# Normalized blocks in the feature maps' buffer, and tail additions moved on VectorE

## The chip, the cores and the metric

The kernel runs on one core of a Trainium2 chip. The metric is the device time of one execution in microseconds (us), the median of the timed runs. The profile is of one further execution on the same kind of chip, taken by the hardware profiler; its times are in us from the first instruction. The engines are PE (TensorE), DVE (VectorE), ACT (ScalarE), POOL (GpSimd) and SP (SyncE), which here only issues DMAs.

## The reference

The input x has 2048 rows of 640 columns, in bfloat16. It is normalized by row, xn = (x - mean) / sqrt(var + 1e-5), and goes into two branches whose product is added back:

```python
def reference(...):
    xn = _layernorm(x, axis=-1)
    s = _A_ref(xn, A_wq, A_wk, A_wv, A_wo, A_beta)                          # attention with a memory
    g = _silu(_B_ref(xn, B_w_gate, B_w_up, B_w_down))                       # gated feed-forward, 640 -> 1536 -> 640
    return x + s * g
```

Branch A has 32 heads of 20 columns and cuts the sequence into 4 segments of 512 rows. In each segment it makes causal softmax attention (a_dot) and a linear read of a memory, num / den with num = phi(q) M and den = phi(q) z, where phi(t) is t + 1 for t > 0 and exp(t) otherwise. The two are mixed by a gate per head; then M and z get this segment's phi(k) and v added. The mixed output is multiplied by wo. Branch B is sigmoid(xn w_gate) * (xn w_up), multiplied by w_down.

## The kernel before

The kernel goes through the 4 segments (n = 0 to 3, 512 rows each). While the attention of segment n runs, slot by slot, the dense work of both branches and the preparation of segment n + 1 are woven in between. The whole order of each engine's instructions is written out by hand: the schedule is manual, an event is put at a slot number with a fraction (the table TIMES), there are 20 slots to a segment, and the PE work that hangs on no due time (gate, up and down products) fills the time between by a planner's costs. So each engine executes its instructions in the order in which the Python code issues them, and a wait of one instruction holds everything behind it on that engine.

Preparing segment m = n + 1 (during segment n): `stats` makes mean and variance, `norm` at slots 5.26, 5.72, 6.03 and 6.29 makes one normalized block of 128 rows each (`ln_norm`, L243, on VectorE), and after each `ln_spill` (L265) stores it from SP's queue into the DRAM scratch Xd, 160 KB. At slot 7.22 `ln_dmaT` (L269) loads all of Xd transposed into xnT. The projections of K (from slot 9.69), Q and V on PE read xnT (L282 and L284 are their evictions).

The normalized blocks lie in a ring of two buffers named xn, so the third and the fourth block of a segment are written into the buffers of the first and the second, after their spills have ended.

The feature maps phi are made in place on ktok and qt by `phi_min` (L360 and L361, VectorE: the minimum with zero into a tile "mn", then the maximum with zero in place), `phi_exp` (L365, ScalarE) and `phi_end` (L369, VectorE). "mn" has one buffer of 1536 columns. In a segment the maps of K come at slots 7.15 to 8.3 and 12.77 to 13.77, those of Q from 16.0 to 19.18. Ahead of segment 0 the same tile serves as the operand of PE's warm-up products.

Gate and up products: `do_gate` ends in a tanh on ScalarE (L421), `do_up` in the product hT on VectorE (L432). `do_down` gives yp on PE, a tanh on ScalarE (L448) and the product aa on VectorE (L449); it is a generator, so that its 12 products can be interleaved with other work. All these accumulate in a ring of four PSUM buffers (tag "d"), which an eviction on ScalarE or VectorE sets free. Attention: `scores` (L541, PE), the exponentials (L549, ScalarE), the masks (L551, GpSimd), the products with V (L565, PE), and then on VectorE the transposes L573 and L585 with the reciprocal L576 between them.

The tail is that of segment 3. The attention output oT (5 chunks of 128 rows) is loaded by L474, L477 and L507 from DRAM, and the memory's part oTm is added by `out_add` (L481): the chunks 0 to 2 at slot 19.86 (one instruction of 1536 columns), chunk 3 at slot 20.9. Chunk 4 is made by `tail_T4` twice, for two blocks of 128 rows each: two transposes on PE (L513), a copy of the lower half by ScalarE (L517), and an addition on VectorE (L518) of o6, which L508 loads. Two down products of the last block of rows ("held") are kept back to give PE work meanwhile. Then come the eight output products of `tail_piece` (L525), each of five matmuls that take the chunks of oT in order, each followed by a product on VectorE (L527), with additions and stores (`tail_add`, L533 and L536).

Of the kernel before, what the change touches and what calls it, by code (L numbers as in the profile page):

```python
# [9 lines left out]
P = 128  # L10
D = 640
# [3 lines left out]
NSEG = 4  # L15
L = 512
F = 1536
DC = D // P
# [6 lines left out]
BF = mybir.dt.bfloat16  # L25
F32 = mybir.dt.float32
ACT = mybir.ActivationFunctionType
ALU = mybir.AluOpType
# [22 lines left out]
def segment_units(n):  # L51
# [6 lines left out]
    turn=(0.03, 0.27, 1.29), turn_last=(0.0, 0.135, 0.43), attend=0.36, last=(0.36, 0.75), rest=350, dot6=0.43, load6=0.48,  # L58
    dot7=1.92, load7=1.95, add=(4.27, 4.52), out=(5.25, 5.95, 7.25, 8.35, 8.74, 9.06, 9.45, 11.05), update=-1.2,
    mem=(2.23, 4.32, 3.0, 6.98, 6.98, 2.45, 9.09, 10.79), mem_spill=11.56, mem_T=14.4, mem_T_last=12.63,  # L60
    k_tok=2.04, dot3=13.22, dot5=17.84, load5=18.1, add5=19.86, dot6_last=19.55, load6_last=19.6, add6_last=20.9, stats0=(0.53, 0.9, 1.65, 3.6),
    stats=(-0.55, 0.13, 1.32, 3.57), norm=(5.26, 5.72, 6.03, 6.29), norm_T=7.22, ready=12.0,
    K=(9.69, 10.07, 10.49, 13.82, 14.29), Q=(11.32, 11.72, 12.29, 12.45, 13.52), K_eng='vaava', Q_eng='avvav',
    V=(10.33, 13.33, 14.43, 14.63, 17.05, 17.66, 19.78, 20.06), V_eng='avaavvav', k_spill0=14.77, k_lay0=15.15,
# [11 lines left out]
def kernel(  # L76
# [14 lines left out]
    nc = tc.nc  # L91
# [5 lines left out]
    ps_d = ctx.enter_context(tc.tile_pool(name="ps_d", bufs=4, space=PSUM))  # L97
    lnp = ctx.enter_context(tc.tile_pool(name="ln", bufs=2))
    stg = ctx.enter_context(tc.tile_pool(name="stg", bufs=1))
# [8 lines left out]
    Xd = [dpool.tile([L, D], BF, name=f"Xd{i}") for i in range(2)]  # L108
# [9 lines left out]
    xt_of, xnT_of = {}, {}  # L118
# [120 lines left out]
        nc.gpsimd.tensor_tensor(rs[:, sl], rs[:, sl], mhalf[:, sl], op=ALU.pow)  # L239

    def ln_norm(n, j, mv, rs):
        xn = lnp.tile([P, D], BF, name="xn", bufs=2)
        nc.vector.tensor_scalar(xn[:], xt_of[n][:, j, :], mv[:, j, 0:1], rs[:, j:j + 1],  # L243
                                op0=ALU.subtract, op1=ALU.mult)
        return xn

    def ln_tiles(n):
        mv = lnp.tile([P, 4, 2], F32, name="mv")
        rs = lnp.tile([P, 4], F32, name="rs")
        return mv, rs  # L250
# [11 lines left out]
            nc.vector.tensor_copy(dst, pT[:])  # L262

    def ln_spill(n, j, xn):
        nc.sync.dma_start(Xd[n % 2][j * P:(j + 1) * P, :], xn[:])  # L265

    def ln_dmaT(n):
        xnT_of[n] = xpool.tile([P, DC, L], BF, name="xnT")
# [2 lines left out]
    seg = {}  # L271
# [181 lines left out]
    def finish(steps):  # L453
        for _ in steps:
            pass
# [23 lines left out]
    def out_add(n, c0, c1):  # L479
        oT = seg[n]["oT"][:, c0:c1, :]  # L480
        nc.vector.tensor_tensor(oT, oT, seg[n]["oTm"][:, c0:c1, :], op=ALU.add)  # L481
# [19 lines left out]
    HALF = P // 2  # L501
    o6 = cpool.tile([HALF, L], BF, name="o6")
    nc.gpsimd.memset(o6[:].bitcast(mybir.dt.uint32), 0)

    def tail_load():
        src = OTd[(NSEG - 1) % 2]
        nc.sync.dma_start(seg[NSEG - 1]["oT"][R5 - C3:P, 3, :], src[R5:C4, :])  # L507
        nc.sync.dma_start(o6[0:R6 - C4, :], src[C4:R6, :])  # L508

    def tail_T4(j0, j1):  # L510
        po = ps_d.tile([P, 2, P], BF, name="po", tag="d")
        for j in range(j0, j1):
            nc.tensor.transpose(po[:, j - j0, :], seg[NSEG - 1]["odot"][:, j, C4:D], ident[:])  # L513
        t = slice(j0 * P, j1 * P)
        oT = seg[NSEG - 1]["oT"][:, DC - 1, t]
        pf = po[:].rearrange("p j t -> p (j t)")
        nc.scalar.copy(oT[HALF:P, :], pf[HALF:P, :])  # L517
        nc.vector.tensor_tensor(oT[0:HALF, :], pf[0:HALF, :], o6[:, t], op=ALU.add)  # L518

    def tail_piece(j, half):  # L520

        s, hs = seg[NSEG - 1], slice(half * HD, (half + 1) * HD)
        sp = ps_d.tile([P, HD], F32, name="sp", tag="d")
        for c in range(DC):
            nc.tensor.matmul(sp[:], lhsT=s["oT"][:, c, j * P:(j + 1) * P], rhs=Wo[:, c, hs],  # L525
                             start=(c == 0), stop=(c == DC - 1), skip_group_check=True)
        nc.vector.tensor_tensor(s["aa"][j][:, hs], s["aa"][j][:, hs], sp[:], op=ALU.mult)  # L527
# [108 lines left out]
    mv, rs = ln_tiles(0)  # L636
# [26 lines left out]
    def norm0(j):  # L663
        if j < 2:
            nc.vector.reciprocal(rs[:, j:j + 1], rs[:, j:j + 1])
        xns[j] = ln_norm(0, j, mv, rs)
# [82 lines left out]
    held = [dense.pop() for _ in range(2)]  # L749
# [9 lines left out]
    def at(t, ns, fn, *a):  # L759
        events.append((t, len(events), ns, lambda: fn(*a)))  # L760

    visits = {}
    for p in range(0, OLD, 5):
        n, g = units[p][0], units[p][1][0][0]
# [36 lines left out]
    def norm(m, j):  # L801
        ln_spill(m, j, ln_norm(m, j, st["mv"], st["rs"]))

    EVAC = dict(v=nc.vector, a=nc.scalar)
    for n in range(NSEG):
        t0 = n * SEG

        def on(name, ns, fn, *items):
            times = TIMES[name]
            for i, it in enumerate(items):  # L810
                at(t0 + (times[i] if isinstance(times, (list, tuple)) else times), ns, fn, *it)

        if n >= 1:
            on("dot6", 0, dot_spill, (n - 1, 4, 7))
            on("load6", 0, out_load, (n - 1, 0, C4))
            on("dot7", 0, dot_spill, (n - 1, 7, 8))
            on("load7", 0, out_load, (n - 1, C4, D))
            if n >= 2:
                on("add", 0, out_add, (n - 1, 0, DC - 1), (n - 1, DC - 1, DC))
            on("out", V_NS, out_item, *[(n - 1, i) for i in range(8)])  # L820
            on("update", 700, m_update, (n - 1,))
            on("mem", MEM_NS, mem_part, *[(n, i % 4, i // 4) for i in range(8)])
            on("mem_spill", 0, mem_spill, (n,))
            on("mem_T_last" if n == NSEG - 1 else "mem_T", 0, mem_T, (n,))
            if n < NSEG - 1:
                on("k_tok", 0, k_tok, (n,))
        on("dot3", 0, dot_spill, (n, 0, 4))
        if n == NSEG - 1:
            on("dot5", 0, dot_spill, (n, 4, 6))
            on("load5", 0, out_load, (n, 0, 6 * 4 * DH))  # L830
            on("add5", 0, out_add, (n, 0, 3))
            on("dot6_last", 0, dot_spill, (n, 6, 7))
            on("load6_last", 0, tail_load, ())
            on("add6_last", 0, out_add, (n, 3, 4))
            continue
        m = n + 1
        on("stats0" if n == 0 else "stats", 0, stats, *[(m, j) for j in range(4)])
        on("norm", 0, norm, *[(m, j) for j in range(4)])
        on("norm_T", 0, ln_dmaT, (m,))
        on("ready", 0, ready.add, (m,))  # L840
        at(t0 + TIMES["K"][0] - 0.001, 0, new_seg, m)
        on("K", GLU_NS, do_K, *[(m, c, EVAC[TIMES["K_eng"][c]]) for c in range(DC)])
        on("Q", GLU_NS, do_Q, *[(m, c, EVAC[TIMES["Q_eng"][c]]) for c in range(DC)])
        on("V", V_NS, do_V, *[(m, i // 2, i % 2, EVAC[TIMES["V_eng"][i]]) for i in range(8)])
        on("k_spill0", 0, spill, (m, 0, nc.sync, None))
        on("k_lay0", 0, relayout, (m, 0, Kd, KT, nc.sync))
        on("q_spill0", 0, spill, (m, 0, None, nc.sync))
        on("q_lay0", 0, relayout, (m, 0, Qd, QT, nc.sync))
        on("q_spill1", 0, spill, (m, 1, None, nc.sync))
        on("k_spill1", 0, spill, (m, 1, nc.sync, None))  # L850
        on("q_abs", 0, q_abs, (m, 0, 3), (m, 3, DC))
        on("bound", 0, bound, (m,))
        on("bound_mm", C_NS, bound_mm, (m,))
        on("bound_lay0", 0, bound_dma, (m, 0))
        at(t0 + SEG - 0.003, 0, relayout, m, 1, Kd, KT, nc.sync)
        at(t0 + SEG - 0.002, 0, relayout, m, 1, Qd, QT, nc.sync)
        at(t0 + SEG - 0.001, 0, bound_dma, m, 1)
        for name, sg, key in (("phi_k", n, "ktok"), ("phi_q", m, "qt")):
            for i, (c0, c1) in enumerate(((0, 2), (2, 4 if key == "ktok" else 5))):
                for fn, t, a in zip((phi_min, phi_exp, phi_end), TIMES[name][i], ((sg, key, c0, c1), (), ())):  # L860
                    at(t0 + t, 0, fn, *a)
        if n + 2 < NSEG:
            on("load_x", 0, load_x, (n + 2,))
# [31 lines left out]
    def fill(want):  # L895
        while done < want and (cur[0] is not None or dense and may(dense[0][0])):
            step()
# [26 lines left out]
        if cur[0] is not None and cur[0][0] * cur[0][1] < TIMES["rest"]:  # L924
            complete()
    fill(1e12)
    for k in (1, 0):
        for _ in range(9):
            next(held[k][3])
        tail_T4(2 - 2 * k, 4 - 2 * k)  # L930
        finish(held[k][3])
    tail_piece(0, 0)
    tail_piece(0, 1)
    tail_add(0, 0, 2, nc.gpsimd, nc.sync)
# [41 lines left out]
```

## Time and profile before

| | |
|---|---|
| median of 3 timed runs | 319.3 us (319.18, 319.30, 320.31) |
| the profiled execution's own time | 320.84 us |
| its span, first to last instruction | 319.0 us |
| mean granted TensorE clock | 0.998 |
| PE busy | 308.1 us, 97% |
| weight loads (beside PE) | 167.8 us, 53% |
| VectorE busy | 226.1 us, 71% |
| ScalarE busy | 226.7 us, 71% |
| GpSimd busy | 134.7 us, 42% |
| DMA | 41.27 MB, mean 129 GB/s |

A line of the list of waits names the waiting engine, the tile and line that it waited to write or run, what released it, and then us in total, how many times, and the longest. A line of the chain in order of time gives its start, its length and what it was; the chain is followed back from the last instruction, at each step to what released it. A line of the timeline gives start, length, engine, line, operation, output and inputs, and in brackets the idle time before it. The ends of matmuls are modelled, so a run of matmuls seems to last somewhat longer than PE needs until the next can start. Engines read a tile's name without its buffer number; "o" in a row of L518 is o6.

### The profile page before, as it was taken

How to read it: one execution, taken by the hardware profiler on the slowest of the kernel's cores; microseconds unless marked ns; L12 is line 12 of the kernel's file. 1: busy time of each engine (PE TensorE's matmuls, PEld its weight loads, DVE VectorE, ACT ScalarE, POOL GpSimd, SP SyncE). 2: the span in 40 equal slices, each digit the busy share in tenths (PEclk: the TensorE clock that was granted, in tenths of full speed). 3: DMA queues.
4: the chain of work that ended last, by engine and by line, in shares of the span. 5: the costliest groups of instructions: out<-in, count | busy, mean ns of one | idle time of the engine just before them, and what ended most of it. 6: DMA issues, size and time to landing. Idle time of an engine off the chain costs nothing.

```text
span 319.0 us, 10222 instructions
## 1 busy us (share of the span) xinstructions
PE 308.1 (97%) x4297; PEld 167.8 (53%) x4327; DVE 226.1 (71%) x507; ACT 226.7 (71%) x228; POOL 134.7 (42%) x231
## 2 busy tenths in 40 slices
PE   7999999989999999899999999999999999999995
PEld 4544445655445445554566454545466655444673
DVE  5474455655868986978869999979686776744475
ACT  3724478769798777767898777678987676777730
POOL 1880035534263444434445364344444353525313
PEclk9999999999999999999999999999999999999999
DMA  7985886230642364513964443419534100180202
GB/s 235 388 312 147 293 216 167 85 84 2 178 151 81 106 123 117 125 43 123 206 177 143 132 104 115 113 69 214 179 94 128 32 23 24 62 165 26 83 23 84
DMA packets 55246, 41.27 MB, mean 129 GB/s; under 512 B 25952, under 2 KB 53824, under 8 KB 55200
## 3 DMA queue, kind: packets, MB, share of 16 engines
q1 hardware_dynamic: 52656, 35.87, 40.8%
q10 hardware_dynamic: 2544, 4.75, 4.0%
q8 instruction: 34, 0.56, 0.7%
q14 instruction: 12, 0.10, 0.1%
HBM read 19.98 MB, written 14.73 MB: 109 GB/s over the span
## 4 chain that ended last, share of the span: by engine, by line
PE 86%; DMA 7%; DVE 3%; issue 1%; ACT 1%; POOL 1%; SPq 0%; DVEq 0%; ACTq 0%
PE up L124 10%; PE psq L124 10%; PE gp L124 9%; PE yp L124 9%; PE Sps L541 8%; PE gp L128 6%; PE up L128 5%; PE ApsT L565 5%; PE psv L124 5%; PE yp L128 4%; PE psq L128 4%; DMA Xd<-xn 4%; PE sp L124 3%; PE psv L128 2%; DMA xnT<-Xd 2%; PE sp L128 2%
## 5 line engine op out<-in xcount | busy, mean ns | idle before, releaser
L549 ACT ACTIVATE pt<-Sps 128x2048 bf16<-128x2048 f32 x80 | 150.2, 1878 | 40.6 <-PE Sps L541 39.8
L551 POOL TENSOR_SCALAR_AFFINE_SELECT pt<-pt 128x512 bf16<-128x512 bf16 x128 | 83.6, 669 | 158.5 <-ACT pt L549 155.8
L432 DVE SCALAR_TENSOR_TENSOR hT<-tg,up 128x512 bf16<-128x512 bf16 x48 | 32.5, 677 | 23.8 <-PE up L124 10.0
L124 PE MATMUL up<-xnT,Wu 128*128 128x512 bf16 x146 | 40.3, 380 | 2.7 <-DVE hT L432 1.3
L124 PE MATMUL gp<-xnT,Wg 128*128 128x512 bf16 x146 | 38.9, 379 | 0.6 <-issue 0.5
L421 ACT ACTIVATE tg<-gp 128x512 bf16<-128x512 f32 x48 | 28.6, 595 | 14.3 <-PE gp L124 10.0
L124 PE MATMUL yp<-Wd,hT 128*128 128x320 bf16 x246 | 38.2, 300 | 0.0
L541 PE MATMUL Sps<-QT,KT 23*128 23x384 bf16 (+3 forms) x512 | 32.1, 301 | 0.1
L124 PEld LDWEIGHTS <-hT 128*128 128x128 bf16 x246 | 22.7, 98 | 11.3 <-issue 3.0
L573 DVE STREAM_TRANSPOSE tb<-ApsT 128x512 f32<-128x512 f32 x31 | 22.0, 710 | 3.4 <-PE ApsT L565 3.3
L128 PE MATMUL gp<-xnT,Wg 128*32 128x512 bf16 x352 | 24.4, 380 | 0.0
L124 PEld LDWEIGHTS <-Wu 128*128 128x128 bf16 x159 | 14.3, 98 | 18.7 <-issue 5.3
L565 PE MATMUL ApsT<-pt,V 128*32 128x512 bf16 (+2 forms) x496 | 23.5, 299 | 0.0
L124 PEld LDWEIGHTS <-Wg 128*128 128x128 bf16 x152 | 14.1, 98 | 15.8 <-issue 1.9
L449 DVE SCALAR_TENSOR_TENSOR aa<-t,yp 128x320 bf16<-128x320 bf16 x32 | 15.2, 475 | 9.8 <-ACT t L448 9.6
L128 PE MATMUL yp<-Wd,hT 128*32 128x320 bf16 x552 | 21.9, 300 | 0.0
L128 PE MATMUL up<-xnT,Wu 128*32 128x512 bf16 x324 | 21.8, 380 | 0.0
L541 PEld LDWEIGHTS <-KT 23*128 23x128 bf16 x512 | 9.3, 92 | 23.6 <-issue 23.4
L585 DVE STREAM_TRANSPOSE obT<-ob 128x256 f32<-128x256 f32 x31 | 13.4, 433 | 11.0 <-POOL ob L582 10.9
L582 POOL TENSOR_TENSOR ob<-tb,rb 128x320 bf16<-128x320 f32 x27 | 19.7, 731 | 2.2
L124 PE MATMUL psq<-xnT,Wq 128*128 128x512 bf16 x82 | 19.4, 379 | 0.2
L124 PE MATMUL psv<-Wv,xnT 128*128 128x320 bf16 x115 | 18.8, 302 | 0.5 <-ACT xnT L661 0.4
(123 smaller groups left out, 444.3 us busy)
## 6 DMA issues: line engine op xcount, KB each, us to landing
KT<-Kd SPq DMA_DIRECT2D x32, 80.0 KB
QT<-Qd SPq DMA_DIRECT2D x32, 80.0 KB
out_dram<-xt SPq DMA_DIRECT2D x14, 160.0 KB
Wg<-in_B_w_gate_dram ACTq DMA_DIRECT2D x1, 1920.0 KB
Wu<-in_B_w_up_dram ACTq DMA_DIRECT2D x1, 1920.0 KB
xt<-in_A_x_dram SPq DMA_DIRECT2D x3, 640.0 KB
Wd<-in_B_w_down_dram SPq DMA_DIRECT2D x1, 1920.0 KB
Xd<-xn SPq DMA_DIRECT2D x12, 160.0 KB
```

What stands on the lines that cost most here:

```text
L124: nc.tensor.matmul(out_, lhsT=lhsT, rhs=rhs, start=start, stop=stop, skip_group_check=True)
L128: nc.tensor.matmul(out_[cols], lhsT=lhsT[:, cols], rhs=rhs, start=start, stop=stop, tile_position=(0, 32 * r), skip_group_check=True)
L421: nc.scalar.activation(tg[:], gp[:], ACT.Tanh, scale=0.5)
L432: nc.vector.scalar_tensor_tensor(out=h[:], in0=seg[n]["tg"][:], scalar=1.0, in1=up[:], op0=ALU.add, op1=ALU.mult)
L449: nc.vector.scalar_tensor_tensor(out=s["aa"][j][:, hs], in0=t2[:], scalar=1.0, in1=yp[:], op0=ALU.add, op1=ALU.mult)
L541: nc.tensor.matmul(Sps[:, r, c0:c0 + ncol], lhsT=KT[32 * r:32 * r + DH + 3, g, kb * P:(kb + 1) * P], rhs=QT[32 * r:32 * r + DH + 3, g, q0: ...
L549: nc.scalar.activation(pt[:, :, 0:ntot], Sps[:, :, 0:ntot], ACT.Exp, scale=SCALE)
L551: nc.gpsimd.affine_select(out=pt[:, :, c0:c0 + P], in_=pt[:, :, c0:c0 + P], compare_op=ALU.is_ge, fill=0.0, base=0, pattern=[[0, 4], [1, P ...
L565: nc.tensor.matmul(ps[32 * r:32 * r + 32, q0:L], lhsT=Vflat[n % 2][:, off:off + 32], rhs=t[:, r, c0:c0 + ncol], start=(i == 0), stop=(i == ...
L573: nc.vector.transpose(tb[:].rearrange("p h e -> p (h e)"), ps[:].rearrange("p (a t b) -> p a b t", t=32, b=2))
L582: eng.tensor_tensor(to, of, by, op=ALU.mult)
L585: nc.vector.transpose(s["obT", g // 4][:, g % 4, :].bitcast(F32), ob[:].rearrange("p a e b -> p (a e b)").bitcast(F32))
```

## The change

Two edits that do not touch each other.

First, for the segments 1 to 3, the first two normalized blocks (j = 0 and 1) are written side by side into one tile "mn" of the feature maps' buffer (2 x 640 of its 1536 columns), taken anew for each segment. The ring of two xn buffers holds the blocks 2 and 3 alone (and all four of segment 0). The spills and the transposing load stay as they are.

Second, in the tail the addition of chunk 3 is taken out of the table of events, and the additions L518 out of `tail_T4`. All three are issued on VectorE after both pairs of transposes and after the end of the first held down product, directly ahead of the end of the second held down product and of the output products.

```diff
     def ln_norm(n, j, mv, rs):
-        xn = lnp.tile([P, D], BF, name="xn", bufs=2)
-        nc.vector.tensor_scalar(xn[:], xt_of[n][:, j, :], mv[:, j, 0:1], rs[:, j:j + 1],
+        if n > 0 and j < 2:
+            if j == 0:
+                seg["xn"] = stg.tile([P, 3 * L], BF, name="mn")
+            xn = seg["xn"][:, j * D:(j + 1) * D]
+        else:
+            xn = lnp.tile([P, D], BF, name="xn", bufs=2)[:]
+        nc.vector.tensor_scalar(xn, xt_of[n][:, j, :], mv[:, j, 0:1], rs[:, j:j + 1],
                                 op0=ALU.subtract, op1=ALU.mult)
         return xn
...
+    tail_po = {}
+
     def tail_T4(j0, j1):
-        po = ps_d.tile([P, 2, P], BF, name="po", tag="d")
+        po = tail_po[j0] = ps_d.tile([P, 2, P], BF, name="po", tag="d")
         for j in range(j0, j1):
             nc.tensor.transpose(po[:, j - j0, :], seg[NSEG - 1]["odot"][:, j, C4:D], ident[:])
+        nc.scalar.copy(seg[NSEG - 1]["oT"][HALF:P, DC - 1, j0 * P:j1 * P],
+                       po[:].rearrange("p j t -> p (j t)")[HALF:P, :])
+
+    def tail_add4(j0, j1):
         t = slice(j0 * P, j1 * P)
-        oT = seg[NSEG - 1]["oT"][:, DC - 1, t]
-        pf = po[:].rearrange("p j t -> p (j t)")
-        nc.scalar.copy(oT[HALF:P, :], pf[HALF:P, :])
-        nc.vector.tensor_tensor(oT[0:HALF, :], pf[0:HALF, :], o6[:, t], op=ALU.add)
+        nc.vector.tensor_tensor(seg[NSEG - 1]["oT"][0:HALF, DC - 1, t],
+                                tail_po[j0][:].rearrange("p j t -> p (j t)")[0:HALF, :], o6[:, t], op=ALU.add)
...
-            on("add6_last", 0, out_add, (n, 3, 4))
...
-    for k in (1, 0):
-        for _ in range(9):
-            next(held[k][3])
-        tail_T4(2 - 2 * k, 4 - 2 * k)
-        finish(held[k][3])
+    for _ in range(9):
+        next(held[1][3])
+    tail_T4(0, 2)
+    finish(held[1][3])
+    for _ in range(9):
+        next(held[0][3])
+    tail_T4(2, 4)
+    out_add(NSEG - 1, 3, 4)
+    tail_add4(0, 2)
+    tail_add4(2, 4)
+    finish(held[0][3])
```

More of the change, by code (lines that the diff above doesn't have):

```diff
@@ L60 @@
     mem=(2.23, 4.32, 3.0, 6.98, 6.98, 2.45, 9.09, 10.79), mem_spill=11.56, mem_T=14.4, mem_T_last=12.63,
-    k_tok=2.04, dot3=13.22, dot5=17.84, load5=18.1, add5=19.86, dot6_last=19.55, load6_last=19.6, add6_last=20.9, stats0=(0.53, 0.9, 1.65, 3.6),
+    k_tok=2.04, dot3=13.22, dot5=17.84, load5=18.1, add5=19.86, dot6_last=19.55, load6_last=19.6, stats0=(0.53, 0.9, 1.65, 3.6),
     stats=(-0.55, 0.13, 1.32, 3.57), norm=(5.26, 5.72, 6.03, 6.29), norm_T=7.22, ready=12.0,
@@ L264, in ln_spill @@
     def ln_spill(n, j, xn):
-        nc.sync.dma_start(Xd[n % 2][j * P:(j + 1) * P, :], xn[:])
+        nc.sync.dma_start(Xd[n % 2][j * P:(j + 1) * P, :], xn)
     def ln_dmaT(n):
```

## The prediction

> **What bounds the kernel now.** I read the page first (busy shares, then the chain that ended last), then who waited for whom, then the chain in order of time around the three places where segments 1 to 3 are normalized, the DMA share there per microsecond, and the timeline of the last 15 us.
>
> ```profile
> PE 308.1 (97%) x4297; PEld 167.8 (53%) x4327; DVE 226.1 (71%) x507; ACT 226.7 (71%) x228; POOL 134.7 (42%) x231
> ```
>
> PE is busy for 308.1 of 319.0 us at a granted clock of 0.998. So work taken off VectorE is worth nothing by itself: only time in which PE stands still can be won, and of the 10.9 us of that some 4.3 lie behind the last product and several more in the start-up. What remains shows in the list of waits (us in total, times, longest):
>
> ```profile
> DVE xn L243 <- DMA Xd<-xn: 4.1, 2, 2.2
> PE up L124 <- DVE hT L432: 1.3, 1, 1.3
> PEld L124 <- DMA xnT<-Xd: 1.3, 1, 1.3
> PE psq L124 <- DMA xnT<-Xd: 0.9, 1, 0.9
> ```
>
> VectorE stands twice, 4.1 us together, at a normalization (L243) until a spill of an earlier block has left the ring of two xn buffers. PE stands once for hT and once for the transposed xnT. The chain in order of time (start us, us, what; three windows, one for each normalization) ties them together:
>
> ```profile
> 55.89 4.30 DMA Xd<-xn
> ...
> 61.49 1.75 DMA Xd<-xn
> ...
> 63.25 6.31 DMA xnT<-Xd
> ...
> 69.61 0.39 PE psq L124
> ...
> 124.11 4.06 DMA Xd<-xn
> ...
> 129.28 0.81 PE up L124 x3
> ...
> 190.87 2.64 DMA Xd<-xn
> ```
>
> The page's chain gives "DMA Xd<-xn" 4%; that is 4.30+1.75+4.06+2.64 = 12.75 us of path, and not what can be won: during most of it PE had other work. What counts is PE's gap at the end of each stretch.
>
> **Part 1: blocks 0 and 1 in the tile mn.** It removes the wait of the third and fourth L243 for the first and second spill. No instruction is added: the same 12 normalizations of 0.45 us, the same 12 spills in the same order on SP.
>
> Segment 0 (which normalizes segment 1). VectorE finished the transpose L573 at 58.04 and then stood 2.24 us. Without that, the four instructions third L243, L576, fourth L243, spill each come 2.24 us earlier: the last spill is issued at about 59.3 in place of 61.49. With its 1.75 us the transposing load starts at about 61.0 and not 63.25. PE's last yp before the gap began its run of six at 67.69; at 0.136 us each (22 in 3.00 us in the chain) it was through at 68.51, and psq started at 69.61: a gap of 1.10 us. The load has to come 1.10 earlier to close it, so the last spill may take up to 62.1-59.3 = 2.8 us. The spills here took 1.75 to 4.30; at 4.30 nothing would be won, at 1.75 all. I take all of it, since the last spill before was the 1.75 one and the DMA share was below a tenth from 58 to 61 us. Bounds 0 to 1.10.
>
> Segment 1. The fourth L243 was ready at 126.37 (L576 ends there) and began at 128.19. Behind it on VectorE is the hT of L432, whose tanh had been ready since about 124.2 and whose product since about 126.2; it began at 128.55, and PE, which needs its PSUM buffer, went on at 129.28. PE's eight score products before that were through at 127.59+0.33 = 127.92: a gap of 1.36 us. With the wait gone hT runs at about 126.75 to 127.45, before PE arrives. Won: 1.36, bounds 0 to 1.36.
>
> Segment 2. The third L243 was held only from 193.40 to 193.54, and three products behind it at 194.63 by at most as much: 0.14.
>
> Sum: 1.10+1.36+0.14 = 2.60 us. All of it passes to the end, because PE runs an order fixed in the program and everything after (projections, spills of K and Q, scores) hangs on PE's own progress and moves along.
>
> The added wait: the first minimum of the feature maps (L360) now takes mn after the blocks, and so waits for both their spills. Queued behind it on VectorE are the maximum L361 and the aa and hT products, on ScalarE the exponential L365. VectorE would get there at about 60.8, 129.1 and 196.9 us; the second spills are issued at about 56.6, 124.1 and 191.6, so they have 4.2, 5.0 and 5.3 us. The longest spill of the trace took 4.30, so the price is 0 to 0.1 us of VectorE, which PE's queued work covers. I take 0.
>
> **Part 2: the tail.** Nothing is added; L481's last addition (0.42 us) and the two L518 (0.28 each) move on VectorE behind the aa of the first held output block. They issue no DMA; the loads they read are issued where they were. PE, ScalarE and SP keep their order. The timeline of VectorE from 307 us shows them in their old places (start us, us, line, operation, in brackets idle time before it and its releaser):
>
> ```profile
> 307.18 0.42 DVE L481 TENSOR_TENSOR oT<-oT,oTm 128x512 bf16<-128x512 bf16 x1
> 307.51 0.48 DVE L449 SCALAR_TENSOR_TENSOR aa<-t,yp 128x320 bf16<-128x320 bf16 x1
> 308.20 0.28 DVE L518 TENSOR_TENSOR oT<-po,o 64x256 bf16<-64x256 bf16 x1 [0.21 <-ACT oT L517]
> 308.68 0.49 DVE L449 SCALAR_TENSOR_TENSOR aa<-t,yp 128x320 bf16<-128x320 bf16 x1 [0.19 <-ACT t L448]
> 309.94 0.28 DVE L518 TENSOR_TENSOR oT<-po,o 64x256 bf16<-64x256 bf16 x1 [0.78 <-ACT oT L517]
> 310.42 0.49 DVE L449 SCALAR_TENSOR_TENSOR aa<-t,yp 128x320 bf16<-128x320 bf16 x1 [0.20 <-ACT t L448]
> ```
>
> PE's row of the same timeline has the 40 output products from 309.75. New order, from these rows: aa to 309.17, L481 to 309.60, first L518 to 309.88, the second still at 309.94 because it waits for ScalarE's copy that ends at 309.91, the last aa at 310.42 as before. The first output product reaches its fourth chunk (L481's) at 309.75+3x0.136 = 310.16 and its fifth (L518's) at 310.29. Margins 0.56 and 0.41 us, and the chain shows PE without a gap up to 314.68: cost 0. If this cover were gone, the three additions together are 0.98 us, of which the margin takes 0.41: at worst 0.57. On the other side, an execution in which the last load lands late holds VectorE less than before; no row shows one, and the smaller wait for the aa ahead frees no PE time. Taken: 0.
>
> **The size.** The profiled execution took 320.84 us (span 319.0 and 1.84 around it), the timed runs 319.18, 319.30 and 320.31. Against its own time the sum gives 320.84-2.60 = 318.2. How much of the 2.60 a median run has is not shown. If recording costs the same everywhere, all: 319.3-2.60 = 316.7. If the 1.54 us between profile and median lie in just these waits, 1.06: 318.2. I take the middle, 317.5. That even the fastest run (319.18) is 0.9 above 318.2 speaks for some of these gaps being there in all runs.
>
> **Rivals.**
> *No change: in timed runs the spills land quickly.* Two of the four spills on the chain took 1.75 and 2.64 us. At these times the first spill of segment 0 lands at 57.6 to 58.5 (needed 58.05) and the second of segment 1 at 125.9 to 126.8 (needed 126.37), so there is next to nothing to remove: 319.3, or 318.9 with what is left. Against it: 4.30 and 4.06 in this execution, and the fastest run that is still 0.9 above the sum. Chance 0.18. On this the Trainium skill, page "DMA: Bandwidth & Descriptors", section "Anatomy of one DMA", has a rule: a nearly constant 2.0 us for each DMA plus bytes over 436 GB/s, given for the GpSimd path. For 160 KB it makes an estimate of 2.4 us, by which waits of 0.3 and 0.1 us would be left and this change would bring nothing; the trace agrees for the 2.64 and differs for the 4.30 and 4.06.
>
> *Slower: the second block waits for the first spill.* If a write to one half of the shared tile counts as a conflict with the DMA that reads the other half, the second L243 waits where the third did. Price: in segment 0 it starts at 60.2 and not 56.14, and with L449 (0.49) and L573 (0.71) still to come the fourth ends at about 63.0, 1.55 later than before; in segment 1 it is held from 123.60 to between 126.0 and 127.65, hT 0.6 to 2.2 later; in segment 2 from 191.12 to 193.5, 2.4 of new wait. Together about 5 us: 324.3. It decides from the moment a spill lasts longer than the 0.25 us to the next normalization, so always. Against it: SP issued the load into oT (L507, 304.93) while L481 was still at work on other columns of that tile (303.86 to 305.20). Chance 0.07. Another 0.05 goes to L360 held by spills longer than the 4.2 us it has, 2 us over the segments: 321.3.
>
> **How the numbers follow.** Forecast case 0.70, between 316.7 and 318.2; no change 0.18; slower 0.12. About 0.5% (1.6 us) is what a measurement of this kernel can tell from no change, so faster means below 317.7: two thirds of the forecast case, 0.47. Within: the rest of it and the no-change rival, 0.41. Slower 0.12. The range runs from 316.7 less 0.3 for the median's own scatter to the no-change time plus 0.4.
>
> **What would show it.** Right: no wait "DVE xn <- DMA Xd<-xn" any more, no PE wait for xnT at about 69 us and for hT at about 128, the transposing load of segment 1 issued near 61, the tail's products without a gap. Wrong: a PE wait for xnT of the same size (last spill slow), a wait of the second L243 for a spill, mn (L360) waiting for Xd<-xn for over a microsecond, or a gap in front of the fourth or fifth chunk of the first output product.

## The result, and the profile after

The changed kernel takes 317.41 us (median of 6 runs, 317.31 to 317.73), the kernel before 319.81 us in the 6 runs set against it. The ratio is 0.9926, 95% interval 0.9911 to 0.9942: 2.4 us less. Its runs also lie closer together: within 0.42 us, where the six of the kernel before spread over 1.3 us. Its profiled execution took 317.50 us with a span of 315.7.

The page's first part shows the same work; PE's share stays at 97% and only the span around it is shorter:

```profile
PE 307.1 (97%) x4297; PEld 167.5 (53%) x4327; DVE 224.9 (71%) x507; ACT 226.6 (72%) x228; POOL 133.5 (42%) x231
```

In the list of waits, the line "DVE xn <- DMA Xd<-xn" is gone, and so are PE's waits for hT and for xnT. These are all of PE's waits that the list names, but for its own issue (us in total, times, longest); all three lie in the start-up:

```profile
PE wps L641 <- DVE mn L149: 1.2, 1, 1.2
...
PE psv L124 <- ACT xnT L670: 0.4, 1, 0.4
...
PE pT L665 <- DVE xn L248: 0.3, 1, 0.3
```

VectorE does not work more for that. It now waits 13.8 us in all for ScalarE's tanh in front of aa, where the same line of the kernel before has 9.6:

```profile
DVE aa L454 <- ACT t L453: 13.8, 18, 1.7
```

That is a wait which holds nobody, in place of one which held PE. The chain in order of time no longer passes through a spill in any of the three stretches. Around the gap of segment 0 (start us, us, what) it is PE alone, and psq begins where yp ends:

```profile
67.26 0.92 PE yp L124 x6
68.18 0.22 PE psq L124
```

The timeline of that stretch shows the third normalization, which had waited, directly behind the transpose L582 on VectorE (the line is L248 now), the fourth behind the reciprocal, and the transposing load that starts at 60.17 in place of 63.25:

```profile
57.48 0.41 DVE L248 TENSOR_SCALAR xn<-xt,mv,rs 128x640 bf16<-128x640 bf16 x1
...
57.96 0.37 DVE L248 TENSOR_SCALAR xn<-xt,mv,rs 128x640 bf16<-128x640 bf16 x1
...
60.17 2.79 SPq L274 DMA_TRANSPOSE xnT<-Xd  x1
60.18 0.87 DVE L365 TENSOR_SCALAR mn<-ktok 128x1280 bf16<-128x1280 bf16 x1
```

L365 is the first minimum of the feature maps, which carries the added wait. It has no idle time before it: the aa ahead of it (59.77, 0.49 us) ends at 60.26 by the record.

In segment 1 hT is made at 124.95 and PE's up products follow the scores at 126.31 without a wait:

```profile
124.68 0.37 DVE L248 TENSOR_SCALAR xn<-xt,mv,rs 128x640 bf16<-128x640 bf16 x1
124.95 0.69 DVE L437 SCALAR_TENSOR_TENSOR hT<-tg,up 128x512 bf16<-128x512 bf16 x1
```

In the tail, the timeline of VectorE has the additions in their new place, and PE's 40 output products start at 306.40. L486 ends at 306.15 and the first L526 at 306.35, and at 0.136 us a product the first output product comes to its fourth chunk at 306.81 and to its fifth at 306.94:

```profile
305.33 0.49 DVE L454 SCALAR_TENSOR_TENSOR aa<-t,yp 128x320 bf16<-128x320 bf16 x1 [1.02 <-ACT t L453]
305.73 0.42 DVE L486 TENSOR_TENSOR oT<-oT,oTm 128x512 bf16<-128x512 bf16 x1
306.07 0.28 DVE L526 TENSOR_TENSOR oT<-po,o 64x256 bf16<-64x256 bf16 x1
306.59 0.28 DVE L526 TENSOR_TENSOR oT<-po,o 64x256 bf16<-64x256 bf16 x1 [0.25 <-ACT oT L521]
307.07 0.49 DVE L454 SCALAR_TENSOR_TENSOR aa<-t,yp 128x320 bf16<-128x320 bf16 x1 [0.20 <-ACT t L453]
```

To see where the time went, I take five marks that every trace has in its chain in order of time: A, the first gate product after 20 us; B, C and D, the first column-split product of the K projection (psq at L128) of segments 1, 2 and 3; and E, the first addition of xt in the tail. B is at 71.60 us before and at 69.99 after. The stretches between marks, in us, of the profiled execution of each kernel (those below the second row are the experiments of the next section):

| kernel | start to A | A to B (segment 0) | B to C (segment 1) | C to D (segment 2) | D to E |
|---|---|---|---|---|---|
| before | 24.98 | 46.62 | 68.57 | 65.71 | 109.35 |
| after | 24.49 | 45.50 | 67.22 | 65.41 | 109.26 |
| part 1 alone | 24.18 | 45.52 | 67.22 | 65.42 | 109.33 |
| part 2 alone | 24.23 | 45.50 | 68.55 | 65.77 | 109.26 |
| part 1, segment 1's blocks | 24.76 | 45.50 | 68.63 | 65.90 | 109.26 |
| part 1, segment 2's blocks | 24.37 | 45.96 | 67.21 | 65.69 | 109.48 |
| blocks in ktd | 24.31 | 45.52 | 67.21 | 65.42 | 109.26 |
| block 0 alone in mn | 24.46 | 45.92 | 68.26 | 65.42 | 109.26 |
| one buffer | 24.39 | 48.76 | 69.92 | 68.86 | 109.32 |
| additions later | 25.33 | 45.52 | 67.22 | 65.41 | 110.55 |
| before, again | 24.26 | 45.53 | 68.55 | 65.74 | 109.26 |
| part 2 alone, again | 24.19 | 45.51 | 68.61 | 65.78 | 109.27 |

From before to after: 0.49 in the start-up, which neither edit touches, 1.12 in segment 0, 1.35 in segment 1, 0.30 in segment 2 and 0.09 in the rest. With the store at the end unchanged, that is the 3.3 us between the two spans.

### The profile page after: what moved, and what is told of

It is laid out like the page before. It is cut to its first block, busy times and chain, and to the rows that moved or that the text cites. A ratio compares the mean times of both kernels' runs of the same rounds, so it can differ in the third digit from the quotient of the medians.

```text
span 315.7 us, 10227 instructions
## 1 busy us (share of the span) xinstructions
PE 307.1 (97%) x4297; PEld 167.5 (53%) x4327; DVE 224.9 (71%) x507; ACT 226.6 (72%) x228; POOL 133.5 (42%) x231
## 4 chain that ended last, share of the span: by engine, by line
PE 95%; DMA 1%; issue 1%; DVE 1%; ACT 1%; SPq 0%; ACTq 0%
PE up L124 11%; PE gp L124 10%; PE yp L124 10%; PE psq L124 10%; PE Sps L550 8%; PE gp L128 6%; PE yp L128 6%; PE up L128 6%; PE ApsT L574 6%; PE psv L124 5%; PE psq L128 4%; PE sp L124 3%; PE sp L128 3%; PE psv L128 2%; PE sp L534 2%; DMA xt<-in_A_x_dram 1%
## 5 line engine op out<-in xcount | busy, mean ns | idle before, releaser
L560 POOL TENSOR_SCALAR_AFFINE_SELECT pt<-pt 128x512 bf16<-128x512 bf16 x128 | 82.5, 660 | 156.6 <-ACT pt L558 153.8
L454 DVE SCALAR_TENSOR_TENSOR aa<-t,yp 128x320 bf16<-128x320 bf16 x32 | 15.3, 478 | 13.9 <-ACT t L453 13.8
L582 DVE STREAM_TRANSPOSE tb<-ApsT 128x512 f32<-128x512 f32 x31 | 22.0, 711 | 4.1 <-PE ApsT L574 4.0
L128 PE MATMUL gp<-xnT,Wg 128*32 128x512 bf16 x352 | 24.4, 380 | 0.0
L128 PE MATMUL yp<-Wd,hT 128*32 128x320 bf16 x552 | 21.9, 300 | 0.0
L128 PE MATMUL up<-xnT,Wu 128*32 128x512 bf16 x324 | 21.7, 380 | 0.0
```

Of the source, the lines that this page charges most:

```text
L128: nc.tensor.matmul(out_[cols], lhsT=lhsT[:, cols], rhs=rhs, start=start, stop=stop, tile_position=(0, 32 * r), skip_group_check=True)
L454: nc.vector.scalar_tensor_tensor(out=s["aa"][j][:, hs], in0=t2[:], scalar=1.0, in1=yp[:], op0=ALU.add, op1=ALU.mult)
L560: nc.gpsimd.affine_select(out=pt[:, :, c0:c0 + P], in_=pt[:, :, c0:c0 + P], compare_op=ALU.is_ge, fill=0.0, base=0, pattern=[[0, 4], [1, P ...
L582: nc.vector.transpose(tb[:].rearrange("p h e -> p (h e)"), ps[:].rearrange("p (a t b) -> p a b t", t=32, b=2))
```

## The experiments

My theory: the gain is PE's gaps behind the two normalizations that wait for spills, segment by segment, and the tail edit is worth nothing. The first rival gives the tail a share; the second says that the spills are slow only in a recorded execution.

**Each part alone.** Part 1 alone is the edit of `ln_norm` and `ln_spill` on the kernel before; part 2 alone the edit of the tail and of its event.

> Part 1 of the change alone (blocks 0 and 1 in mn, the tail as before). My theory: the whole gain is PE's gaps behind the two spill waits, 1.10 us in segment 0, 1.36 in segment 1 and 0.2 in segment 2, so 2.3 to 2.7 us under the kernel before, the same time as the full change within 0.3 us. Rival: the tail has a share of the 2.4 us measured; then 1.4 to 1.9 us under the kernel before.

Measured: 317.41 us (median of 12 runs), ratio 0.9935 (0.9914 to 0.9955). That is the time of the full change, and the stretches A to D agree with it within 0.02 us. The theory holds, and no share is left for the tail.

> Part 2 of the change alone (the three tail additions moved, the normalized blocks as before). My theory: no change, within 0.4 us of the kernel before, and PE without a gap in the tail. Rival: 0.5 to 1.0 us faster, because in most executions the last loads of the tail land late and hold VectorE; or up to 0.57 us slower, if the additions come too late for the fourth and fifth chunk.

Measured: 319.29 us (12 runs), ratio 0.9963 (0.9940 to 0.9986), 0.57 us less than the median of the kernel before: outside what I expected, and inside the rival's 0.5 to 1.0. Its trace speaks against a gain of its own, since D to E is 109.26 and the kernel before has 109.35; the unrelieved losses of segments 1 and 2 are there in full (68.55 and 65.77). What is short is segment 0, where this execution lost nothing. So I had the kernel before timed against itself, with part 2 once more beside it.

> The kernel before, unchanged, timed against itself. It shows how far two sets of runs of one program differ by chance, with the length of the spills, the start-up and the profile left to scatter. If the lower median of the tail edit alone (319.29 against 319.86) is such scatter, this one may differ from the kernel before by as much, up to 0.5 us either way. If the tail edit has a gain of its own, this one should lie within 0.2 us of the kernel before.

> Part 2 of the change alone once more, on the same chip as the kernel before timed against itself. My theory (the tail edit does nothing, and the run before was lucky in its spills): within 0.4 us of both. Rival (a gain of its own): again 0.5 us or more under both, while the output products start nearer to the projections of segment 3 in its trace than the 105.3 to 105.4 us of all kernels so far.

Measured: the unchanged kernel 320.50 us against 319.69, ratio 1.0013 (0.9984 to 1.0042); part 2 alone 319.55, ratio 1.0002 (0.9977 to 1.0027). The same program differs from itself by 0.8 us between the medians of 12 and 23 runs, more than the 0.5 I had allowed and more than part 2 differed, and part 2's lower time did not come again: it lies 0.14 us from one set of runs of the kernel before and 0.95 from the other. Its stretch D to E is 109.27, that of the unchanged kernel 109.26. The tail edit does nothing that these runs can show.

**One segment at a time.** The condition of the edit is cut to one segment:

```diff
-        if n > 0 and j < 2:
+        if n == 1 and j < 2:      # the other kernel: n == 2
```

> Part 1 for segment 1 alone (normalized during segment 0; segments 2 and 3 keep the ring of two). My theory: the gap of 1.10 us in front of the first psq goes, the gap of hT in segment 1 stays: 0.8 to 1.2 us under the kernel before. Rival (the spills are slow only while a profile is recorded, and quick in timed runs): under 0.4 us.

> Part 1 for segment 2 alone (normalized during segment 1; segments 1 and 3 keep the ring of two). My theory: the gap of 1.36 us in front of the up products near 128 us goes, that near 69 us stays: 1.1 to 1.5 us under the kernel before; with the kernel that has it for segment 1 alone it adds up to part 1 within 0.4 us. Rival (the spills are slow only while a profile is recorded): under 0.4 us.

Measured: 319.00 us for segment 1's blocks (ratio 0.9971, 0.9959 to 0.9984) and 318.58 for segment 2's (0.9964, 0.9946 to 0.9982), against 319.86: 0.9 and 1.3 us less. Both as the theory says, and together 2.1 of the 2.4 to 2.5 us of part 1; the rest is segment 2's stretch, with its 0.3. In the stretches each kernel has its own segment at the level of the changed kernel (45.50; 67.21) and the others not. The gaps are thus there in timed runs too. For segment 0 this rests on the timed runs alone: the stretch of 45.50 also stands in executions that leave its ring in place, and 0.9 us is little more than the 0.8 by which the unchanged kernel differs from itself.

The trace of the first of them shows the gap of segment 1 that it leaves in place (chain in order of time):

```profile
122.85 3.65 DMA Xd<-xn
126.50 0.03 issue
126.52 0.03 DVE xn L248
126.55 0.63 issue
127.19 0.68 DVE hT L437
```

**Another buffer than mn.** All four blocks go into the buffer of the K projection, which is not written until the first eviction of K:

```diff
-        xn = lnp.tile([P, D], BF, name="xn", bufs=2)
+        if n > 0:
+            if j == 0:
+                seg["xn"] = stg.tile([P, DC, L], BF, name="ktd")
+            xn = seg["xn"][:].rearrange("p c n -> p (c n)")[:, j * D:(j + 1) * D]
+        else:
+            xn = lnp.tile([P, D], BF, name="xn", bufs=2)[:]
```

> The kernel before with all four normalized blocks of segments 1 to 3 in the buffer of the K projection (ktd, 4 x 640 of its 2560 columns, free until the first eviction of K at slot 9.69), tail as before. It takes the spill waits away without touching mn. My theory (the gain is only the spill waits): the same 2.3 to 2.7 us as part 1 with mn, within 0.3 us of it. Rival (mn's new wait at L360 costs something, hidden in the net gain): 0.4 us or more faster than part 1 with mn.

Measured: 317.47 us, ratio 0.9934 (0.9916 to 0.9953), 2.4 us less and within 0.1 us of part 1 with mn; the stretches are equal to 0.02 us. So mn itself is not what matters, and the wait that it adds at the first minimum has no price.

**Half of the relief.** The condition `j < 1` leaves block 1 in the ring, so that only the third normalization is free of the spills.

> The kernel before with block 0 alone in mn; the blocks 1, 2 and 3 go through the ring of two, so that the fourth normalization still waits for the spill of block 1. My theory: segment 0 wins little, since the spill of block 1 lands within 0.7 us of that of block 0, and segment 1 nothing, since there the wait was for block 1: 0 to 0.6 us under the kernel before. Rival (any one relieved block is enough): 2 us or more.

Measured: 319.12 us, ratio 0.9976 (0.9960 to 0.9993), 0.7 us less. Just beyond the 0.6 of the theory and far from the rival. Segment 1 keeps most of its loss (68.26 against 67.22, so 1.04 of 1.35); segment 0 keeps 0.42 us; segment 2 loses nothing any more (65.42), which I had not separated: in this trace it was the third normalization alone that had cost.

**More waiting.** Blocks 1 to 3 are written into block 0's buffer, so that each normalization waits for the spill ahead of it:

```diff
-        xn = lnp.tile([P, D], BF, name="xn", bufs=2)
+        if n > 0 and j > 0:
+            xn = seg["xn"]
+        else:
+            xn = seg["xn"] = lnp.tile([P, D], BF, name="xn", bufs=2)[:]
```

> The kernel before with a single buffer for the four blocks of segments 1 to 3: the second, third and fourth normalization each wait for the spill just ahead. The waits become three for each segment. My theory: VectorE is held three times 1.75 to 4.3 us in each segment, the transposing load of segment 0 starts some 5 us later, and PE's gaps grow by 3 to 6 us in each segment: 10 to 18 us slower. Rival (VectorE's waits hardly reach PE): under 5 us slower.

Measured: 327.22 us, ratio 1.0236 (1.0203 to 1.0270), 7.4 us slower. Between the two: the sign and the mechanism are right, the size was too large. VectorE waits 13.4 us for spills where the kernel before had 4.1, and the stretches A to D stand 3.26, 2.70 and 3.45 us above the changed kernel's. I had put each wait at 1.75 to 4.30 us; the chain of segment 0 shows why most are shorter:

```profile
55.30 3.52 DMA Xd<-xn
...
58.92 0.46 DVE xn L246
...
59.40 1.77 DMA Xd<-xn
...
61.74 1.75 DMA Xd<-xn
...
64.50 1.74 DMA Xd<-xn
```

The later spills are through in 1.74 to 1.77 us, at the lower end of what I had put in, and the eight waits make 1.7 us each. And VectorE waits less elsewhere: 10.4 us for ScalarE's tanh in front of aa, where the changed kernel has 13.8.

**The tail's margin.** The full change with the three additions moved behind the last aa:

```diff
     tail_T4(2, 4)
+    finish(held[0][3])
     out_add(NSEG - 1, 3, 4)
     tail_add4(0, 2)
     tail_add4(2, 4)
-    finish(held[0][3])
```

> The full change, but with the three tail additions behind the aa of the second held block in place of ahead of it. By the changed kernel's rows that aa ends at 307.56, the additions would follow to 307.98, 308.26 and 308.54, and PE needs the fourth and fifth chunk at 306.81 and 306.94: a gap of 1.2 to 1.4 us in the first output product, and the time 1.2 to 1.4 us above the full change (about 318.7). Rival (PE takes other products meanwhile or the margins were misread): within 0.4 us of the full change.

Measured: 318.66 us (12 runs), 1.25 us above the full change, as worked out from its rows. The stretch D to E grows by 1.29. The timeline shows PE stopping in the first output product after three chunks, until L486 has made the fourth:

```profile
308.34 0.42 DVE L486 TENSOR_TENSOR oT<-oT,oTm 128x512 bf16<-128x512 bf16 x1
308.68 0.48 DVE L526 TENSOR_TENSOR oT<-po,o 64x256 bf16<-64x256 bf16 x2
308.82 3.43 PE L534 MATMUL sp<-Wo,oT 128*128 128x320 bf16 x23 [0.98 <-DVE oT L486]
```

So the times at which PE needs its chunks, read from modelled matmul rows, were right to about 0.1 us, and the place chosen for the additions lies one instruction ahead of where they begin to cost.

## Why the prediction was right

317.5 us was forecast and 317.41 measured. By its steps:

*Only PE's gaps count.* Right. VectorE's 4.1 us of waiting were worth 2.8 us between the marks, and the 12.75 us of spills on the chain no more than that.

*Segment 0, 1.10 us.* 1.12 in the two profiled executions. The condition, a last spill of under 2.8 us, held: the last spill was issued after the fourth normalization at 57.96 and the transposing load started at 60.17. But this term scatters from run to run. Other executions with the ring unchanged lost 0.46 (segment 2's blocks relieved), 0.03 (before, again), 0.00 (part 2 alone) and 0.01 (the same again), so that the profile to be predicted from happened to have the largest loss of the five. VectorE's wait for the first spill was 2.24 us there, 1.73 where 0.46 was lost, and 1.10 to 1.35 in the other three: some 1.1 to 1.3 us of it are covered by PE's work. The bounds of 0 to 1.10 were the right thing to give, but the reason for taking all of it was not: the DMA share was below a tenth from 58 us on while the long spill was still under way. The last section shows what the long spills have in common.

*Segment 1, 1.36 us.* 1.35. This one does not scatter: 1.33 to 1.41 in the five traces that leave it in place.

*Segment 2, 0.14 us.* 0.30; the term was sized too small. I counted only the time for which VectorE stood before the third normalization. PE's own gap in front of the memory products was 0.21 by the rows that I had, and the marks show 0.30 (0.28 to 0.49 in the unrelieved traces).

*The added wait at the first minimum, 0.* Right: no wait in the trace, and the same time with the blocks in a buffer that the first minimum does not use.

*The tail, 0.* Right. The margins forecast as 0.56 and 0.41 us are 0.66 and 0.59 in the changed kernel's rows, and the kernel that oversteps them pays 1.29.

*The size in timed runs.* The weak step. I halved between two readings, one in which recording costs the same everywhere (2.60 us won) and one in which the 1.54 us between the profile and the median lie in these waits (1.06). Recording costs nothing that shows: the unchanged kernel, recorded again, took 318.96 us, less than its median. The first recorded execution was simply a long one, with 0.72 us more in the start-up and 1.09 more in segment 0 than the second. The gain of the medians is 2.4 us, near the upper reading; the forecast had 1.8. That the time still came out within 0.1 us is luck: the three runs shown had a median of 319.30, half a microsecond under the later 319.7 to 319.9, and the two errors cancel. How the 2.4 is shared out in timed runs is known in part only: 1.35 and 0.30 leave some 0.75 for segment 0 (an estimate), where the five traces lost 0.3 on average.

*The rivals.* "No change" would have needed spills of 1.75 to 2.64 us. No trace has them in front of these two waits. Where segment 0 lost nothing, the third normalization still stood 1.10 to 1.35 us for the first spill, and PE's queued work covered it. Segment 1's second spill took 4.06, 3.52, 3.65, 3.71 and 4.09 us in the five traces that leave its wait in place. On this the Trainium skill, page "DMA: Bandwidth & Descriptors", section "Anatomy of one DMA", gives a nearly constant 2.0 us and the bytes on top, by its table for the GpSimd path; the estimate of 2.4 us that follows for 160 KB is above the 1.75 us of the short spills and far under the 3.5 to 4.1 us of segment 1. The other rival, a second block that waits for the first spill, did not happen: the second normalization of segment 0 starts at 55.65 with the first spill issued at 55.40. What it would have cost was not tried by itself; three such waits for each segment cost 7.4 us.

## What to carry to other kernels

When an engine works in order and reuses a buffer that a DMA still reads, the price is not its own wait but the work queued behind it for the bottleneck engine; look for the bottleneck's gap at the end of that chain and add up the gaps. A buffer that is idle in that phase removes such a wait, whatever its name: two different ones gave the same time here (a larger ring was not tried). Its own next use has to be checked for the wait that moves there. Before crediting half a per cent to an edit, time the unchanged program against itself, and compare the stretches of the traces that the edit can touch.

## What the runs showed of the hardware

One and the same spill of 160 KB from SP's queue took 1.74 to 1.79 us eight times out of the ten that stand on the chain of the kernel with one buffer, where a spill is done before the next is issued. The other two, each the first of its segment, took 3.52 and 3.05 us. In the kernels with the ring of two, those that the chain passes through and that held VectorE took 2.6 to 4.3 us. The stages of one microsecond show where such a long one, issued at 55.30, spends its time (one buffer, segment 0; us, then busy share and instructions of PE, PEld, DVE, ACT and POOL, the granted clock, the DMA share and GB/s):

```profile
56.00:57.00 1.00, 1.00 (x31) 0.47 (x22) 0.00 (x0) 0.22 (x1) 0.00 (x0) 1.00 0.51 170
57.00:58.00 1.00, 1.00 (x12) 0.73 (x9) 0.00 (x0) 0.56 (x1) 0.00 (x0) 1.00 0.04 5
58.00:59.00 1.00, 1.00 (x10) 0.69 (x8) 0.08 (x1) 1.00 (x1) 0.00 (x0) 1.00 0.05 13
```

Most of the bytes move in one microsecond, and the DMA engines then stand nearly idle while the spill is still not done. The DMA view tells whose bytes they are (queue and kind: packets, MB, share of 16 engines; the first two lines for 56 to 57 us, the others for 57 us to the spill's end at 58.83):

```profile
q1 hardware_dynamic: 135, 0.15, 41.9%
q8 instruction: 1, 0.02, 8.7%
...
q1 hardware_dynamic: 9, 0.01, 3.0%
q14 instruction: 1, 0.01, 1.7%
```

The spill is 128 packets of 1280 bytes and 16 of 4 bytes. Of these, 120 and 15 move in the first microsecond. The remaining eight and one are a sixteenth of the whole, the share of one of the 16 DMA engines if they share evenly. By the trace's record of packets, the one packet of kind "instruction" (16 KB) starts at 56.15 and takes 1.40 us, and the late eight start at 57.55, when it ends. In the kernel before, the same kind of packet runs from 56.98 to 58.90 in segment 0, the late eight of the first spill begin at 58.88, and the third normalization starts at 60.28.

This holds throughout. The chains of all the kernels here pass through 17 spills of 2.6 to 4.3 us and 11 of 1.74 to 1.79 us. Each of the 17 has such an instruction packet of 1.0 to 1.9 us under way, and ends 1.2 to 1.8 us after it; none of the 11 has one while its own bytes move. It also fits the scatter of segment 0: in the five executions that leave its ring in place, the packet ended 3.0, 2.4 and three times 2.2 us after the first spill was issued, and the losses were 1.12, 0.46 and 0.00 to 0.03 us. This is read from the traces; no run here moved those packets.
